# Strided-head loads laid out as (row of 32, group), split over two queues, a mask from a one-hot product, and filler products at the start

## The chip, the cores and the metric

One core of one Trainium2 chip runs the whole program. The metric is the device time of one execution in microseconds (us). It is the median over several executions of the same compiled kernel. Profiled executions are separate ones: their rows give the durations, and their own total stands beside their span below.

## What is computed

The program is an attention layer followed by two gated feed-forward layers, all in float32:

```
scores = (1/sqrt(D)) * q @ k.T                     # 4 batches, 8 heads, 576 positions, D = 64
rel = pos[:, None] - pos[None, :]
mask_local   = (rel >= 0) & (rel < 32)             # heads 0..3
mask_strided = (rel >= 0) & (pos[None] % 32 == pos[:, None] % 32)   # heads 4..7
attn = softmax(where(mask, scores, -1e9)) ;  x = attn @ v           # heads side by side: 2304 x 512
x = x / sqrt(mean(x*x) + 1e-6) * rms_g
x = (silu(x @ w_gate) * (x @ w_val)) @ w_out       # d_ff = 1536
out = (silu(x @ w2_gate) * (x @ w2_val)) @ w2_out
```

What matters here are the strided heads. A position is 32 t + r, with t from 0 to 17 (the row of 32) and r from 0 to 31 (the residue). A query sees only keys of its own residue and of rows t up to its own.

## The kernel before, in words

**Strided heads in groups.** The kernel packs several residues into one tile of positions, so that one 126x126 or 108x108 product gives the scores of many residues at once; a mask takes away pairs of different residues. Residues 0 to 29 are written as r = 5 a + g, with a from 0 to 5 and g from 0 to 4. Group g holds the six residues a, each with its 18 rows t: 108 positions. The two residues 30 and 31 are put behind groups 0 and 1 as positions 108 to 125, so those two groups have 126 positions. In the kernel before, position index is (a, t), a outside and t inside. `load_strided` (L550) loads one tensor of one batch with five DMAs: one per head of 108 runs of 320 floats (L555) and one for residues 30 and 31 (L557). In batch 0 two of k's five are issued from GpSimd (POOL), all others from SyncE (SP), in the order q, k, v.

**Order of a batch.** `batch` (L899) writes the steps of a batch in a list: six transposes of q and k (`strided_t`, L631, operation at L80) into `qT` and `kT`, copied out of PSUM at L87; then per group a score step (`strided_s`, product at L76), a softmax (maximum with mask at L675 on VectorE, exp at L684 on ScalarE, normalising at L701 on GpSimd), a transpose of the weights (`turn_step`) and the product with v (`strided_v`, L797), whose `post` (L813) copies the result from PSUM into the tile `x` with the residues put back in place. The local heads follow. The loads of the local heads of a batch reuse the tiles of its strided q and k (L573), so they wait for the last transpose that reads these.

**What else runs in the first 50 us.** The steps of the attention of batch 0 are mixed with the decoding of the first weights: `raw` tiles are loaded on SP (L160), scaled on ScalarE (L288, L280, L305) and joined on VectorE (L292, L297, L309). A scheduler with a model of its own then fixes the order of the instructions on each engine; each engine takes its instructions in that order.

**Fillers.** `keep_busy` (L67) counts the steps with products or transposes at the start of the program. At the counts in a small table it puts in products of a constant tile `warm` (128x128 by 256 columns), whose result nobody reads (L72). In the kernel before the first are at count 11.

**Constants.** `consts` (L531) builds the masks on GpSimd with `affine_select`: two local masks, `ms` for the strided heads (index j not above i, and j in the same run of 18 as i), then `ones`, and `warm` as a copy of it on VectorE (L546).

After some 250 us only the feed-forward layers are left, as a long sequence of products on TensorE (PE), with weights fetched and split beside them.

Of the kernel before, what the change touches and what calls it, by code (L numbers as in the profile page):

```python
# [12 lines left out]
ALU = mybir.AluOpType  # L13
# [4 lines left out]
NEG = -8.0e9  # L18
# [7 lines left out]
def attn_ffn_ffn(ctx: ExitStack, tc: tile.TileContext, q, k, v, w1g, w1v, w1o, rms_g, w2g, w2v, w2o, out):  # L26
    nc = tc.nc
    B, H, S, D = q.shape
# [4 lines left out]
    HH = H // 2  # L33
# [33 lines left out]
    def keep_busy():  # L67
        if state["start"] and state["kind"] and state["group"] != state["filled"]:
            state["filled"] = state["group"]
            state["count"] += 1  # L70
            for _ in range({11: 24, 14: 8, 28: 5, 31: 7, 34: 9, 36: 22}.get(state["count"], 0)):
                traced(nc.tensor.matmul(att.fill, att.warm[:, :128], att.warm, start=True, stop=True))  # L72

    def product(out_, a, b_, start, stop, **how):
# [7 lines left out]
    def bank(tag):  # L82
        return pp.tile([128, 512], F32, tag=tag, name=f"b_{tag}")

    def copy(eng, out_, in_):
        if eng is nc.scalar:
            nc.scalar.copy(out=out_, in_=in_)  # L87
        else:
            eng.tensor_copy(out=out_, in_=in_)
# [405 lines left out]
    class Attention:  # L495
# [35 lines left out]
        def consts(self):  # L531
            g = nc.gpsimd

            def sel(t, pattern, base, cm):
                g.affine_select(out=t, in_=t, pattern=pattern, compare_op=ALU.is_ge, fill=NEG, base=base, channel_multiplier=cm)

            for m, leads in ((self.m0, (0, 32)), (self.m1, (32, 32))):
                g.memset(m, 0.0)
                for par, lead in enumerate(leads):
                    sel(m[64 * par:64 * par + 64], [[-1, 96]], lead, 1)  # L540
                    sel(m[64 * par:64 * par + 64], [[1, 96]], 31 - lead, -1)
            g.memset(self.ms, 0.0)
            sel(self.ms, [[-1, 126]], 0, 1)
            sel(self.ms, [[18, 7], [0, 18]], 17, -1)
            g.memset(self.ones, 1.0)
            nc.vector.tensor_copy(out=self.warm.rearrange("p (a k) -> p a k", a=2), in_=self.ones.unsqueeze(1).to_broadcast([128, 2, 128]))  # L546
            g.memset(self.expo, -0.5)
            nc.sync.dma_start(out=self.gcol, in_=rms_g.rearrange("(c p) -> p c", p=128))

        def load_strided(self, t, src, b, engs=None):  # L550

            engs = engs or [nc.sync] * 5
            for h in range(HH):
                s = src[b, HH + h].rearrange("(t r) d -> t r d", r=32)[:, 0:30, :].rearrange("t (a g) d -> a t (g d)", g=5)
                engs[h].dma_start(out=t[0:108, h].rearrange("p (g d) -> p g d", d=D), in_=s)  # L555
            s = src[b, HH:H].rearrange("h (t r) d -> t h r d", r=32)[:, :, 30:32, :].rearrange("t h r d -> t h (r d)")
            engs[4].dma_start(out=t[108:126, :, 0:2 * D], in_=s)  # L557

        def load(self, b, half):
            res = []  # L560
            for nm, src in (("q", q), ("k", k)):
                if half == 0:
                    t = self.p1.tile([128, 5, HH * D], F32, tag=nm, name=f"{nm}n{b}{half}")
                else:
                    t = self.p1.tile([126, HH, 5 * D], F32, tag=nm, name=f"{nm}n{b}{half}")
                    self.load_strided(t, src, b, [nc.sync,nc.sync,nc.gpsimd,nc.gpsimd,nc.sync] if b == 0 and nm == "k" else None)
                res.append(t)
            self.ld[b, half] = res
            if half == 0:
                for h in range(0, HH, 2):  # L570
                    for t, src in zip(res, (q, k)):
                        for h_ in (h, h + 1):
                            nc.sync.dma_start(out=t[:, 0:4, h_ * D:(h_ + 1) * D], in_=src[b, h_, 0:512].rearrange("(c p) d -> p c d", p=128))  # L573
                for t, src in zip(res, (q, k)):
                    nc.sync.dma_start(out=t[0:64, 4].rearrange("p (h d) -> p h d", d=D),
                                      in_=src[b, 0:HH, 512:S].rearrange("h p d -> p h d"))

        def load_v(self, b, half):
# [10 lines left out]
                nc.sync.dma_start(out=t[:, :, 0, :], in_=v[b, 0:HH, 0:96, :].rearrange("h p d -> p h d"))  # L589
            else:  # L590
                t = self.p1.tile([126, HH, 5 * D], F32, tag="vs", name=f"vs{b}")
                self.load_strided(t, v, b)
            self.vt[b, half] = t

        def qk_tile(self, b, half, which):
# [201 lines left out]
        def strided_v(self, b, part, pair):  # L797
            cell = {}
# [13 lines left out]

            def post():  # L813
                x = self.x_tile(b, 1)
                nr = n // 18
                for k in range(2):
                    g = 2 * part + k if pair is not None else 4
                    d = x[:, k if pair is None else pair].rearrange("p (t r) -> p r t", r=32)[:, g:g + 5 * (nr - 1) + 1:5, :]
                    copy(self.eng(), d, cell["o"][:, 128 * k:128 * k + n].rearrange("p (r t) -> p r t", t=18))

            return Step([pe, post] + ([lambda: self.squares(b, 0)] if part == 2 else []),
                        lambda: ("T", ("s", b, part, pair)) in self.st and (b == 0 or (b - 1, 1) in self.done), kind="v")
# [277 lines left out]
    open_pool("px", "px", 0, bufs=1)  # L1100
    actx = ExitStack()
    att = Attention(actx)
    make_identity(nc, att.ident)
    att.load(0, 1)
    att.load_v(0, 1)
# [611 lines left out]
```

## Time and profile before

| | us |
|---|---|
| median of 3 runs | 1014.53 (1012.96 to 1014.74) |
| the profiled execution, its own time | 1019.0 |
| span of its rows | 1017.2 |
| PE busy | 970.2 (95%) |
| VectorE (DVE) busy | 582.4 (57%) |
| ScalarE (ACT) busy | 578.1 (57%) |
| GpSimd (POOL) busy | 387.6 (38%) |

The profiled execution took 4.5 us more than the median of the runs; 1.8 us of its time lie outside its span. Rows of the trace are in us from the start of the span. Busy times are sums of durations that may overlap on one engine. In the chain of work that ended last, traced back from the end, PE holds 71% of the span.

### The profile page before, as it was taken

The numbers are of one execution on the slowest core, as the hardware profiler recorded it, in microseconds if no ns is written. First come the engines' busy times: TensorE is split into PE (matmuls) and PEld (weight loads), VectorE is DVE, ScalarE is ACT, GpSimd is POOL, SyncE is SP. The second block draws the span as 40 slices with busy tenths as digits, with TensorE's granted clock in tenths as the row PEclk, the third lists the DMA queues.
The fourth block names the chain that finished last, engine by engine and source line by source line (L and its number), as shares of the span: only waits on it lengthen the run. The fifth ranks groups of instructions, "written<-read, shape, count | busy, mean of one in ns | idle before, by whom it ended". The sixth has DMA issues, their size and how long they took to land.

```text
span 1017.2 us, 17631 instructions
## 1 busy us (share of the span) xinstructions
PE 970.2 (95%) x5987; PEld 891.7 (88%) x5987; DVE 582.4 (57%) x1310; ACT 578.1 (57%) x1465; POOL 387.6 (38%) x417
## 2 busy tenths in 40 slices
PE   5789988899999999998999999999999999999998
PEld 4678966667889999998999999999998999999997
DVE  2887766767244656455655566554556645653333
ACT  5988675675254646354655555555646555663431
POOL 3221243442050538160716464673517143431500
PEclk9989999799999999999999999999999999999999
DMA  7774647856777474977567777637887397865211
GB/s 184 216 228 139 162 134 230 240 173 212 257 262 260 147 231 167 318 258 266 188 203 249 277 227 247 202 135 285 281 285 244 133 303 247 311 199 181 83 63 63
DMA packets 167794, 215.87 MB, mean 212 GB/s; under 512 B 46356, under 2 KB 121308, under 8 KB 167704
## 3 DMA queue, kind: packets, MB, share of 16 engines
q1 hardware_dynamic: 158296, 199.79, 60.7%
q10 hardware_dynamic: 9216, 14.68, 3.9%
q8 instruction: 47, 0.77, 0.3%
q14 instruction: 43, 0.35, 0.1%
q0 software_dynamic: 192, 0.28, 0.1%
HBM read 142.87 MB, written 71.83 MB: 211 GB/s over the span
## 4 chain that ended last, share of the span: by engine, by line
PE 71%; DMA 3%; ACT 2%; DVE 1%; issue 0%; SPq 0%; DVEq 0%; ACTq 0%
PE b_y L76 32%; PE b_a L76 17%; PE b_g L76 12%; PE b_v L76 10%; DMA pk<-dh 1%; DMA w<-pk 1%; DMA raw<-in_moe_w_gate_dram 0%; DMA pk<-raw 0%; ACT xh L1389 0%; ACT dh L280 0%; ACT hh L1471 0%; ACT raw L288 0%; DVE dh L297 0%; ACT t L1447 0%; ACT t L1461 0%
## 5 line engine op out<-in xcount | busy, mean ns | idle before, releaser
L1390 POOL TENSOR_TENSOR xl<-xst,xh 128x384 fp32r<-128x384 f32 x196 | 211.4, 1100 | 179.7 <-PE b_y L76 77.6
L76 PE MATMUL b_y<-xh,w 128*128 128x384 f32 x784 | 212.1, 336 | 5.0 <-ACT t L1447 3.1
L76 PEld LDWEIGHTS b_y<-xh,w 128*128 128x128 f32 x784 | 143.5, 188 | 8.2 <-ACT t L1447 3.7
L76 PE MATMUL b_a<-xh,w 128*128 128x384 f32 (+2 forms) x512 | 141.3, 336 | 0.8 <-ACT t L1447 0.7
L76 PE MATMUL b_y<-xl,w 128*128 128x384 f32 x392 | 131.7, 336 | 0.0
L76 PE MATMUL b_g<-xh,w 128*128 128x384 f32 (+2 forms) x416 | 127.9, 349 | 0.0
L76 PE MATMUL b_v<-xh,w 128*128 128x384 f32 (+2 forms) x352 | 109.3, 353 | 1.8 <-ACT t L1461 1.8
L76 PEld LDWEIGHTS b_a<-xh,w 128*128 128x128 f32 x512 | 93.3, 188 | 4.4 <-ACT t L1447 2.0
L1389 ACT CAST xh<-xst 128x384 fp32r<-128x384 f32 x196 | 91.6, 521 | 0.3 <-DMA xst<-y_d 0.3
L386 POOL TENSOR_TENSOR raw<-dh 128x256 f32<-128x256 f32 x40 | 29.4, 754 | 154.5 <-ACT t L1447 36.8
L76 PE MATMUL b_a<-xl,w 128*128 128x384 f32 (+2 forms) x256 | 85.9, 335 | 0.0
L76 PEld LDWEIGHTS b_g<-xh,w 128*128 128x128 f32 x416 | 77.4, 191 | 5.3 <-issue 0.4
L76 PE MATMUL b_y<-hh,w 128*128 128x384 f32 (+2 forms) x304 | 81.4, 343 | 0.0
L76 PEld LDWEIGHTS b_y<-xl,w 128*128 128x128 f32 x392 | 73.7, 188 | 1.8
L76 PEld LDWEIGHTS b_v<-xh,w 128*128 128x128 f32 x352 | 65.8, 193 | 7.4 <-ACT t L1461 2.2
L701 POOL TENSOR_TENSOR e<-e,rc 128x384 f32<-128x384 f32 (+3 forms) x40 | 35.8, 903 | 93.8 <-DVE rc L695 28.0
L76 PE MATMUL b_g<-xl,w 128*128 128x384 f32 (+2 forms) x208 | 70.8, 340 | 0.0
L76 PE MATMUL b_y<-w,hh 128*128 128x512 f32 x216 | 67.1, 391 | 0.0
L684 ACT ACTIVATE e<-e,nb 128x96 f32<-128x96 f32 (+2 forms) x152 | 56.8, 380 | 9.7 <-DVE nb L675 8.7
L76 PE MATMUL b_v<-xl,w 128*128 128x384 f32 (+2 forms) x176 | 60.3, 342 | 0.0
L76 PEld LDWEIGHTS b_y<-hh,w 128*128 128x128 f32 x304 | 55.2, 190 | 2.7
L1467 DVE TENSOR_TENSOR b_y<-b_y,t 128x384 f32<-128x384 f32 x56 | 31.6, 565 | 44.4 <-ACT b_y L1461 43.4
(206 smaller groups left out, 2149.7 us busy)
## 6 DMA issues: line engine op xcount, KB each, us to landing
w<-pk SPq DMA_DIRECT2D x48, 512.0 KB
raw<-in_moe_w_gate_dram SPq DMA_DIRECT2D x24, 512.0 KB
raw<-in_moe_w_val_dram SPq DMA_DIRECT2D x24, 512.0 KB
raw<-in_moe_w_out_dram SPq DMA_DIRECT2D x24, 512.0 KB
pk<-raw ACTq DMA_DIRECT2D x48, 256.0 KB
part<-ob SPq DMA_DIRECT2D x48, 256.0 KB
xst<-y_d SPq DMA_DIRECT2D x30, 384.0 KB
xst<-xq SPq DMA_DIRECT2D x28, 384.0 KB
```

The costliest lines, as they stand in the source:

```text
L76: traced(nc.tensor.matmul(out_, a, b_, start=start, stop=stop, **how))
L386: paced(nc.gpsimd.tensor_tensor(out=t[:, z], in0=a, in1=b, op=ALU.subtract))
L684: r = nc.scalar.activation(out=e[:qn, i, :kn], in_=e[:qn, i, :kn], func=AF.Exp, bias=nb[:qn, i:i + 1], scale=-1.0, accum_out=sums[:qn, i:i ...
L701: eng.tensor_tensor(out=e[:qn, :nt, :kn], in0=e[:qn, :nt, :kn], in1=rc[:qn, :nt].unsqueeze(2).to_broadcast([qn, nt, kn]), op=ALU.mult)
L1389: nc.scalar.copy(out=xh[:, kk], in_=src[:, kk])
L1390: paced(nc.gpsimd.tensor_tensor(out=xl[:, kk], in0=src[:, kk], in1=xh[:, kk].bitcast(F32), op=ALU.subtract), ("pe", None))
L1467: nc.vector.tensor_tensor(out=s, in0=s, in1=v, op=ALU.mult)
```

## The change

- **Index (t, a) instead of (a, t).** Position in a group is now 6 t + a. `load_strided` loads, per head, rows t = 0 to 15 with one DMA whose source runs over 16 rows, 6 residues and 320 floats; rows 16 and 17 come with one DMA each for all four heads together (6 residues x 4 heads x 320 floats); residues 30 and 31 as before. That is seven DMAs a tensor instead of five.
- **Two queues in batch 0.** k's seven are issued from ScalarE, q's and v's from SP, none from GpSimd.
- **Mask by product.** Seven one-hot rows (six for a, one for residues 30 and 31) are built on 7 partitions; their product with themselves on PE is 1 where residues agree; VectorE turns that into 0 or -8e9, and one `affine_select` on GpSimd sets the upper triangle.
- **Result copies.** `strided_v` copies 108 columns per group to `x` as (t, a). In groups 0 and 1 one more copy on VectorE for both groups together puts residues 30 and 31 in place.
- **Products of constants at the top.** `ones` and `warm` are made first of all constants, and `keep_busy` puts 22 filler products ahead of the first transpose.

```
--- before.py
+++ after.py
@@ -68,7 +68,7 @@
         if state["start"] and state["kind"] and state["group"] != state["filled"]:
             state["filled"] = state["group"]
             state["count"] += 1
-            for _ in range({11: 24, 14: 8, 28: 5, 31: 7, 34: 9, 36: 22}.get(state["count"], 0)):
+            for _ in range({1: 22, 11: 24, 14: 8, 28: 5, 31: 7, 34: 9, 36: 22}.get(state["count"], 0)):
                 traced(nc.tensor.matmul(att.fill, att.warm[:, :128], att.warm, start=True, stop=True))
 
     def product(out_, a, b_, start, stop, **how):
@@ -531,30 +531,32 @@
         def consts(self):
             g = nc.gpsimd
 
-            def sel(t, pattern, base, cm):
-                g.affine_select(out=t, in_=t, pattern=pattern, compare_op=ALU.is_ge, fill=NEG, base=base, channel_multiplier=cm)
-
+            def sel(t, pattern, base, cm, op=ALU.is_ge, fill=NEG):
+                g.affine_select(out=t, in_=t, pattern=pattern, compare_op=op, fill=fill, base=base, channel_multiplier=cm)
+
+            row = self.ms[0:7]
+            g.memset(row, 0.0)
+            sel(row[:, 0:108].rearrange("p (t a) -> p t a", a=6), [[0, 18], [-1, 6]], 0, 1, ALU.not_equal, 1.0)
+            sel(row[:, 108:126], [[0, 18]], -6, 1, ALU.not_equal, 1.0)
+            same = bank("g")
+            nc.tensor.matmul(same[0:126, 0:126], row, row, start=True, stop=True)
+            nc.vector.tensor_scalar(out=self.ms[0:126], in0=same[0:126, 0:126], scalar1=1.0, scalar2=-NEG, op0=ALU.subtract, op1=ALU.mult)
             for m, leads in ((self.m0, (0, 32)), (self.m1, (32, 32))):
                 g.memset(m, 0.0)
                 for par, lead in enumerate(leads):
                     sel(m[64 * par:64 * par + 64], [[-1, 96]], lead, 1)
                     sel(m[64 * par:64 * par + 64], [[1, 96]], 31 - lead, -1)
-            g.memset(self.ms, 0.0)
-            sel(self.ms, [[-1, 126]], 0, 1)
-            sel(self.ms, [[18, 7], [0, 18]], 17, -1)
-            g.memset(self.ones, 1.0)
-            nc.vector.tensor_copy(out=self.warm.rearrange("p (a k) -> p a k", a=2), in_=self.ones.unsqueeze(1).to_broadcast([128, 2, 128]))
+            sel(self.ms[0:126], [[-1, 126]], 0, 1)
             g.memset(self.expo, -0.5)
             nc.sync.dma_start(out=self.gcol, in_=rms_g.rearrange("(c p) -> p c", p=128))
 
-        def load_strided(self, t, src, b, engs=None):
-
-            engs = engs or [nc.sync] * 5
+        def load_strided(self, t, src, b, eng):
+            s = src[b, HH:H].rearrange("h (t r) d -> t h r d", r=32)
             for h in range(HH):
-                s = src[b, HH + h].rearrange("(t r) d -> t r d", r=32)[:, 0:30, :].rearrange("t (a g) d -> a t (g d)", g=5)
-                engs[h].dma_start(out=t[0:108, h].rearrange("p (g d) -> p g d", d=D), in_=s)
-            s = src[b, HH:H].rearrange("h (t r) d -> t h r d", r=32)[:, :, 30:32, :].rearrange("t h r d -> t h (r d)")
-            engs[4].dma_start(out=t[108:126, :, 0:2 * D], in_=s)
+                eng.dma_start(out=t[0:96, h], in_=s[0:16, h, 0:30].rearrange("t (a g) d -> t a (g d)", g=5))
+            for i in (16, 17):
+                eng.dma_start(out=t[6 * i:6 * i + 6], in_=s[i, :, 0:30].rearrange("h (a g) d -> a h (g d)", g=5))
+            eng.dma_start(out=t[108:126, :, 0:2 * D], in_=s[:, :, 30:32].rearrange("t h r d -> t h (r d)"))
 
         def load(self, b, half):
             res = []
@@ -563,7 +565,7 @@
                     t = self.p1.tile([128, 5, HH * D], F32, tag=nm, name=f"{nm}n{b}{half}")
                 else:
                     t = self.p1.tile([126, HH, 5 * D], F32, tag=nm, name=f"{nm}n{b}{half}")
-                    self.load_strided(t, src, b, [nc.sync,nc.sync,nc.gpsimd,nc.gpsimd,nc.sync] if b == 0 and nm == "k" else None)
+                    self.load_strided(t, src, b, nc.scalar if b == 0 and nm == "k" else nc.sync)
                 res.append(t)
             self.ld[b, half] = res
             if half == 0:
@@ -589,7 +591,7 @@
                 nc.sync.dma_start(out=t[:, :, 0, :], in_=v[b, 0:HH, 0:96, :].rearrange("h p d -> p h d"))
             else:
                 t = self.p1.tile([126, HH, 5 * D], F32, tag="vs", name=f"vs{b}")
-                self.load_strided(t, v, b)
+                self.load_strided(t, v, b, nc.sync)
             self.vt[b, half] = t
 
         def qk_tile(self, b, half, which):
@@ -812,11 +814,13 @@
 
             def post():
                 x = self.x_tile(b, 1)
-                nr = n // 18
                 for k in range(2):
                     g = 2 * part + k if pair is not None else 4
-                    d = x[:, k if pair is None else pair].rearrange("p (t r) -> p r t", r=32)[:, g:g + 5 * (nr - 1) + 1:5, :]
-                    copy(self.eng(), d, cell["o"][:, 128 * k:128 * k + n].rearrange("p (r t) -> p r t", t=18))
+                    d = x[:, k if pair is None else pair].rearrange("p (t r) -> p t r", r=32)
+                    copy(self.eng(), d[:, :, g:g + 26:5], cell["o"][:, 128 * k:128 * k + 108].rearrange("p (t r) -> p t r", r=6))
+                if part == 0:
+                    copy(nc.vector, d[:, :, 30:32].rearrange("p t r -> p r t"),
+                         cell["o"][:, 0:256].rearrange("p (k n) -> p k n", n=128)[:, :, 108:126])
 
             return Step([pe, post] + ([lambda: self.squares(b, 0)] if part == 2 else []),
                         lambda: ("T", ("s", b, part, pair)) in self.st and (b == 0 or (b - 1, 1) in self.done), kind="v")
@@ -1100,6 +1104,8 @@
     open_pool("px", "px", 0, bufs=1)
     actx = ExitStack()
     att = Attention(actx)
+    nc.gpsimd.memset(att.ones, 1.0)
+    nc.vector.tensor_copy(out=att.warm.rearrange("p (a k) -> p a k", a=2), in_=att.ones.unsqueeze(1).to_broadcast([128, 2, 128]))
     make_identity(nc, att.ident)
     att.load(0, 1)
     att.load_v(0, 1)
```

On PE, the start of the program, before the first transposes of q (`qn`) and k (`kn`) of the strided heads. Before:

```order
L1712 UNCONDITIONAL_BRANCH
L80 MATMUL b_a_162<-ident,qn_107 128x126 x4
L80 MATMUL b_a_171<-ident,kn_113 128x126 x4
L80 MATMUL b_g<-ident,qn_107 128x108 x4
L80 MATMUL b_y_186<-ident,kn_113 128x108 x4
```

After:

```order
L1718 UNCONDITIONAL_BRANCH
L72 MATMUL b_v<-warm 128x256 x21
L542 MATMUL b_g<-ms 126x126
L72 MATMUL b_v<-warm 128x256
L80 MATMUL b_a_174<-ident,qn_109 128x126 x4
L80 MATMUL b_a_205<-ident,kn_117 128x126 x4
L80 MATMUL b_g<-ident,qn_109 128x108 x4
```

The fillers and the mask's product stand ahead of the transposes; behind them the order on PE is the same to the end of the program, but for one group of eight score products.

On ACT, the start of the program, ahead of the first copies of transposes out of PSUM. After (before, the first row here is the table load, and no DMA stands on this engine):

```order
L556 DMA kn_117<-in_k_dram 96x1x320 x4
L558 DMA kn_117<-in_k_dram 6x4x320 x2
L559 DMA kn_117<-in_k_dram 18x4x128
L87 ACT_TABLE_LOAD
L87 COPY qT_201<-b_a_174 128x504
```

Seven issues now stand ahead of the table load.

On DVE, the softmax of the strided heads of the last batch, between the sums (`sums`), their reciprocals (`rc`) and the gate of a feed-forward block (`sg`). Before:

```order
L694 TENSOR_SCALAR sums<-sums 126x4
L695 RECIPROCAL rc<-sums 126x4
L694 TENSOR_SCALAR sums<-sums 108x4
L695 RECIPROCAL rc<-sums 126x4
L695 RECIPROCAL rc<-sums 108x4
L972 SCALAR_TENSOR_TENSOR sg<-sg,b_g 128x512
L694 TENSOR_SCALAR sums<-sums 108x4
L695 RECIPROCAL rc<-sums 108x4
L89 COPY pT<-b_a_2888 126x4x126
```

After:

```order
L434 TENSOR_TENSOR raw<-raw 128x512
L697 RECIPROCAL rc<-sums 126x4
L696 TENSOR_SCALAR sums<-sums 126x4
L696 TENSOR_SCALAR sums<-sums 108x4
L697 RECIPROCAL rc<-sums 126x4
L697 RECIPROCAL rc<-sums 108x4
L696 TENSOR_SCALAR sums<-sums 108x4
L697 RECIPROCAL rc<-sums 108x4
L89 COPY pT<-b_a_2946 126x4x126
L976 SCALAR_TENSOR_TENSOR sg<-sg,b_g 128x512
```

A subtraction of a weight (`raw`) now stands ahead of the reciprocals, and the gate behind the copy of `pT`.

## Rows read from the trace of the kernel before

**Rows 1.** The page's busy times of the engines, share of the span.

```profile
PE 970.2 (95%) x5987; PEld 891.7 (88%) x5987; DVE 582.4 (57%) x1310; ACT 578.1 (57%) x1465; POOL 387.6 (38%) x417
```

**Rows 2.** Windows of 50 us: length, busy by engine, PE's granted clock, DMA share, GB/s.

```profile
0.00:50.00 50.00, 32.39 (x357) 27.57 (x357) 27.92 (x121) 38.17 (x132) 15.00 (x34) 1.00 0.73 198
...
150.00:200.00 50.00, 41.46 (x264) 31.77 (x265) 32.80 (x103) 31.03 (x97) 17.44 (x21) 0.86 0.81 245
```

**Rows 3.** Timeline, PE, first transposes and scores: start, length, operation, [idle before, releaser].

```profile
8.98 1.07 PE L80 MATMUL b_a<-ident,qn 126*128 126x126 f32 x4 [8.98 <-DMA qn<-in_q_dram]
11.05 1.07 PE L80 MATMUL b_a<-ident,kn 126*128 126x126 f32 x4 [0.99 <-DMA kn<-in_k_dram]
...
14.07 0.93 PE L80 MATMUL b_y<-ident,kn 108*64 108x108 f32 x4
14.93 0.57 PE L76 MATMUL b_y<-kT,qT 64*126 64x126 f32 x1
```

**Rows 4.** Timeline, SP, DMA issues of the first 16 us.

```profile
0.75 3.30 SPq L555 DMA_DIRECT2D qn<-in_q_dram  x4
...
6.72 3.06 SPq L555 DMA_DIRECT2D vs<-in_v_dram  x4
...
10.81 0.49 SPq L160 DMA_DIRECT2D raw<-in_moe_w_gate_dram  x1
...
14.31 0.92 SPq L573 DMA_DIRECT2D qn<-in_q_dram  x2
```

**Rows 5.** Windows, columns as in rows 2: strided loads alone, and other loads.

```profile
8.00:13.00 5.00, 3.03 (x15) 2.69 (x16) 0.00 (x0) 1.28 (x3) 0.00 (x0) 1.00 0.43 149
14.00:18.00 4.00, 4.00 (x45) 3.57 (x44) 2.00 (x19) 2.81 (x10) 0.00 (x0) 1.00 1.05 360
```

**Rows 6.** DMA view, 0 to 30 us in 40 slices; issue to landing of POOL's k loads.

```profile
DMA  0003466444544444488999999999999792389898
...
DMA to landing us min/median/max: 3.9/4.2/4.4
```

**Rows 7.** Timeline, ACT, from the start to the first decoded weight.

```profile
0.74 1.28 ACT L87 ACT_TABLE_LOAD   x1 [0.74 <-PEq L1701]
...
16.33 0.40 ACT L684 ACTIVATE e<-e,nb 126x126 f32<-126x126 f32 x1 [0.78 <-DVE nb L675]
...
16.73 0.65 ACT L288 ACTIVATE raw<-raw 128x512 uint32<-128x512 uint32 x1
```

**Rows 8.** Timeline, constants, fillers and later transposes.

```profile
3.83 0.40 DVE L546 CAST warm<-ones 128x256 fp32r<-128x256 f32 x1 [3.83 <-POOL ones L545]
...
17.12 3.12 PE L72 MATMUL b_v<-warm 128*128 128x256 f32 x24
...
21.88 0.65 PE L80 MATMUL b_a<-ident,e 126*126 126x126 f32 x4 [1.64 <-POOL e L701]
...
57.12 0.53 PE L80 MATMUL b_y<-ident,qn 108*64 108x108 f32 x4
57.49 0.53 PE L80 MATMUL b_y<-ident,kn 108*64 108x108 f32 x4
```

**Rows 9.** Timeline, copies of results on ACT and small operations on DVE.

```profile
28.67 0.60 ACT L87 COPY x<-b_y 128x126 f32<-128x126 f32 x2
...
19.41 0.17 DVE L694 TENSOR_SCALAR sums<-sums 126x4 f32<-126x4 f32 x1
...
201.64 0.28 DVE L89 COPY qT<-b_y 128x128 f32<-128x128 f32 x1
```

**Rows 10.** Timeline, PE, the last batch's two longest waits.

```profile
179.11 0.48 PE L76 MATMUL b_y<-kT,qT 64*126 64x126 f32 x1 [2.32 <-DVE mean L864]
188.72 0.65 PE L80 MATMUL b_a<-ident,e 126*126 126x126 f32 x4 [2.44 <-POOL e L701]
```

**Rows 11.** Windows of 4 us, columns as in rows 2, behind the second wait.

```profile
188.00:192.00 4.00, 3.27 (x15) 2.73 (x16) 2.83 (x12) 1.79 (x9) 4.00 (x5) 0.68 1.01 346
192.00:196.00 4.00, 4.00 (x14) 2.76 (x14) 0.35 (x2) 1.46 (x7) 1.26 (x2) 0.50 0.93 284
```

## The prediction

> **What bounds the kernel now.** I read the page's busy times first, then the windows, then the timeline of the first 20 us engine by engine, and last the waits of the middle. PE is busy 95% of the span [rows 1]. The missing time is not spread evenly: in the first 50 us PE is busy 32.39 us, in 150 to 200 us 41.46 [rows 2]. So some 17.6 us of idle PE lie at the start and 8.5 in one later stretch, and the rest of the program is PE back to back. A shorter start moves everything behind it by as much, unless something there has a time of its own.
>
> At the start PE has nothing to do until q has landed, at 8.98, and then waits 0.99 more for k, which lets it go on at 11.05; the first score product starts at 14.93 [rows 3]. SP issues q's four large DMAs in 3.30 us, so 0.8 us each, and v's only from 6.72; the first weight is issued at 10.81 and the local heads' q at 14.31 [rows 4], which is just behind the last transpose of the strided q. While only strided loads run, 8 to 13 us, the DMA engines are 0.43 busy at 149 GB/s; with weights and local heads in flight, 14 to 18 us, they are full at 360 GB/s [rows 5]. The row of forty slices of 0.75 us shows the same: nothing before slice 4, then a long row of 4s, then 9s [rows 6]. So the strided loads keep 6 or 7 of 16 engines busy. A shortage of bytes is not what makes PE wait.
>
> ACT starts on its first exp at 16.33 and on its first weight at 16.73 [rows 7]; from there to 50 us it is close to full (38.17 of 50 us with the empty first 10, [rows 2]). ACT, in order, sets the pace of the head once it has begun.
>
> **The change, part by part.**
>
> *Loads of q and k.* The source now runs over 16 rows outside, where it ran over 6 residues. I take it that these loads then spread like the weights' in 14 to 18 us, 0.43 to full. A tensor of strided heads is 4 heads x 576 rows x 64 floats = 0.59 MB, so q and k are 1.18 MB. At 149 GB/s they need 7.9 us, at 360 GB/s 3.3 us [rows 5]. Issue: bounds 0.8 us each (q's own, [rows 4]) and 0.49 (a weight's, which spreads, [rows 4]); I take 0.5 because the new form spreads. Seven cost 3.5 us from 0.75, on SP for q and on ACT for k side by side; the last is issued from 3.75 on (with 0.8: 5.55). From issue to landing: POOL's k loads took 3.9 to 4.4 us on the crowded six engines [rows 6], the upper bound; the lower is 1.9, between the first issue at 0.75 and the slice in which the first DMA moves, the fourth, whose middle is 2.6 us. I take 2.65, nearer the low end, since the crowd goes: q and k land at 6.4. The data alone gives 2.6 + 3.3 = 5.9, so it agrees; ends 5.65 and 8.15 (0.5 issue with the shorter landing, 3.75 + 4.4; the dear issue with 2.65 gives 8.2).
>
> The Trainium skill (DMA: Bandwidth & Descriptors, Issuing engines are not separate DMA queues) says that a second issuing engine saves only the issue time, which it calls usually small beside the DMA. Here the rows say otherwise: 3.30 us of issue for 0.49 MB, where 360 GB/s would move that in 1.4. By the page the data would set the landing, 5.9 instead of my 6.4, and the gain would be 0.5 us more.
>
> *ACT's seven issues* (3.5 us) stand ahead of its table load of 1.28 us [rows 7]: 0.75 + 3.5 + 1.28 = 5.5, before the first copy that ACT has to make, at 7 us. Cost nothing; with the dear issue 7.6, half a us late.
>
> *Fillers and transposes.* Four transposes of 126 columns take 1.07 us at the start, and 0.65 later, as part of the same kernel; of 108 columns 0.93 and 0.53 [rows 3, 8]. The granted clock reads 1.00 in 8 to 13 us [rows 5], yet the operations take 1.7 times as long, so I trust the durations: the first transposes ran at the lower level, 1.2 GHz. The 22 fillers shall change that. `ones` moves from behind two DMA issues on POOL to the front, so `warm`, cast at 3.83 [rows 8], is there at about 1.5. A filler takes 0.13 us at the higher level (24 in 3.12, [rows 8]), up to 0.26 at the lower: 22 end between 4.4 and 7.2, say 6.0, when q lands. After a wait of 1.64 us PE still ran at the higher level [rows 8], so a short gap loses nothing. Before, five groups take 3.88 us from 11.05 to the first score [rows 3]; now all six wait for nothing but PE: 4.7 at the lower level, and by 0.53/0.93 to 0.65/1.07, so 0.6, 2.8 at the higher. First score: 6.4 + 2.8 = 9.2 instead of 14.93, **5.7 us earlier**. Ends: at the lower level, with fillers to 7.2, 11.9, so 3.0; landing at 8.2 and the lower level 12.9, so 2.0; landing at 5.65 and the higher level 8.45, so 6.5.
>
> *Mask.* Its product stands as the 22nd on PE; POOL makes its rows before, and behind it come one operation on DVE and one on POOL, both idle then. The scores need it 3 us later. Nothing; if it were late, it would be late by tenths.
>
> *What follows the first score.* v's issues end at 0.75 + 14 x 0.5 = 7.75, so the first weight goes out at 8.2 instead of 10.81, 2.6 us earlier, on engines that are then nearly free of strided data: before, the 1.77 MB of q, k and v took 11.9 us at 149 GB/s, from 2.6 to 14.5. At 360 GB/s the 0.52 MB are there at 8.2 + 1.9 + 1.5 = 11.6. ACT would reach it behind its third exp at 16.33 - 5.7 + 1.2 = 11.8 [rows 7]. The local heads' q goes out when SP is through with three weights, at 11 instead of 14.31, 3.3 earlier. So the loads just keep up; I take off 0.4 for one of them that does not (between 0 and 3, the latter if loads alone set the pace).
>
> *Result copies.* ACT copies 108 columns a group instead of 126 (two in 0.60, [rows 9]), with another order of the addresses: not dearer on a row here, and a seventh fewer columns. The eight new copies on DVE move 36 floats a lane: between 0.17 (a tiny operation) and 0.28 (128 columns) each [rows 9], 1.4 to 2.2 us in all, of which a quarter falls in batch 0's full stretch. DVE is 27.92 of 50 busy there, so at most 0.5 is on the path; I take 0.3.
>
> *Loads of batches 1 to 3.* Two more issues a tensor, each dearer by at most 7 x 0.5 against 5 x 0.7; SP is not what PE waits for. They also stop crowding 6 engines. No wait of PE in 40 to 260 us ends on a DMA, so I give it nothing, and the surplus to a rival.
>
> **Sum:** 5.7 - 0.4 - 0.3 = 5.0 us. Against the profiled execution 1019.0 - 5.0 = 1014.0; this execution was 4.5 above the median of the runs, and the same difference from that gives 1014.5 - 5.0 = **1009.5**, its own range 1008 to 1011.
>
> **The rivals.** *The lower clock stays* (0.15). For it: nothing in rows 3 shows a rise before 14.93. Against: fillers ran 0.13 us each later. Gain 3.0 - 0.7 = 2.3: 1012.2.
>
> *The loads set the pace* (0.12): the weights and local heads go out only 2.6 and 3.3 us earlier, and ACT, in order, stands before the first weight with all exps behind it. Or the new form does not spread, and q and k land at 2.6 + 7.9 = 10.5, the first score at 13.3. Either way 1 to 2 us: 1013.0. Against it speaks the full 360 GB/s of loads that run over 128 rows outside, and ACT's full row once it has begun, which is why it stays low. The Trainium skill (DMA: Bandwidth & Descriptors, Why a DMA increments its semaphore by 16 and not by 1) has the number of engines as the largest up to 16 that divides both outer sizes: 6 before (residues) and 16 after. The trace agrees for before (0.43 x 16 = 6.9); of after it has no row.
>
> *Batch 3 loses its clock more often* (slower, 0.14 with its mild form). In the last batch's softmax DVE has a new order: a weight's subtraction ahead of the reciprocals. PE waits there already 2.32 and 2.44 us [rows 10], and behind the second the granted clock is 0.68 and then 0.50 [rows 11], which is 0.32 x 4 + 0.5 x 4 = 3.3 us lost; in all of 150 to 200 us 0.14 x 50 = 7.0 [rows 2]. One more fall eats 3.3 of the 5.0: 1012.8, no change (0.06). If the shifted start makes the stretch lose its 7.0 a second time, the kernel is slower by 2.0 and more: 1016.6 (0.08). It decides from two added falls on. For it: the order of DVE and ACT changes up to there. Against: the order on PE does not.
>
> *More than the start* (0.09): strided loads that no longer crowd six engines also shorten waits in batches 1 to 3, 2 to 3 us: 1007.
>
> **How the numbers follow.** My forecast has 0.50. About 0.2% (2 us) is what a measurement of this kernel can tell from no change. Faster: 0.50 + 0.15 + 0.09 = 0.74; within: 0.12 + 0.06 = 0.18; slower: 0.08. The range takes in the first four cases and the ends of the landing and the clock: 6.5 with a surplus of 3 at one end (1005), a gain of nothing at the other (1014.6); what is left out is the slower case and some of the largest gain.
>
> **What would show it.** Right: first transpose at about 6.4 with 0.65 us for four, first score at 9 to 9.5, first exp at 10.6, full DMA share by 5 us, and PE's later rows the same but earlier by 5. Clock wrong: transposes of 1.07 us. Loads: ACT waiting before L288. Batch 3: a PE wait above 2.5 us near 180, and a granted clock below 0.8 in 150 to 200. The prediction fails if the first score comes 5 us earlier and the end does not.

## The result, and the profile after

| | before | after |
|---|---|---|
| median of 5 runs, us | 1014.53 (1012.89 to 1016.18) | 1006.85 (1002.65 to 1007.29) |
| ratio, 95% interval | | 0.9917 [0.9893, 0.9941] |
| the profiled execution, us | 1019.0 | 1006.85 |

The change saves 7.7 us by the medians. The predicted 1009.5 is 2.7 us off and the range holds the result, but the gain does not come from where I put it: the first score comes only 0.7 us earlier, and the new form in batches 1 to 3 alone, to whose loads I gave nothing, gains as much as the whole change.

The page's busy times and the two windows of the kernel after, which answer to [rows 1, 2]:

```profile
PE 974.6 (97%) x6011; PEld 897.3 (89%) x6011; DVE 579.1 (58%) x1319; ACT 576.9 (57%) x1465; POOL 387.2 (39%) x416
```

```profile
0.00:50.00 50.00, 39.16 (x382) 33.81 (x382) 27.43 (x124) 38.54 (x133) 14.86 (x33) 0.90 0.77 200
150.00:200.00 50.00, 44.00 (x323) 33.46 (x320) 36.32 (x114) 32.71 (x104) 20.66 (x23) 0.93 0.82 252
```

PE is busy 6.77 us more in the first 50 us than before, but some 4.6 us of that are fillers, so it is no shorter start. In 150 to 200 us it is busy 2.54 us more at a higher granted clock (0.93 for 0.86); that is work done earlier.

**The start.** PE's timeline of the kernel after (answers to [rows 3, 8]):

```profile
1.59 4.21 PE L72 MATMUL b_v<-warm 128*128 128x256 f32 x21 [1.59 <-DVE warm L1108]
...
9.53 1.07 PE L80 MATMUL b_a<-ident,qn 126*128 126x126 f32 x4 [3.00 <-DMA qn<-in_q_dram]
10.40 1.05 PE L80 MATMUL b_a<-ident,kn 126*128 126x126 f32 x4
...
13.40 0.93 PE L80 MATMUL b_y<-ident,kn 108*64 108x108 f32 x4
14.26 0.57 PE L76 MATMUL b_y<-kT,qT 64*126 64x126 f32 x1
```

The fillers start at 1.59 and end at 6.53. Then PE waits 3.00 us for q, which is there at 9.53, later than the 8.98 of before, and the transposes take 1.07 us as before. Only k no longer has a wait of its own. The first score comes at 14.26 instead of 14.93. Why q is late stands in the issues of SP and, behind them, of ACT (answers to [rows 4, 7]):

```profile
0.74 2.91 SPq L556 DMA_DIRECT2D qn<-in_q_dram  x4
3.69 2.88 SPq L558 DMA_DIRECT2D qn<-in_q_dram  x2
6.71 0.27 SPq L559 DMA_DIRECT2D qn<-in_q_dram  x1
```

```profile
0.73 2.63 ACTq L556 DMA_DIRECT2D kn<-in_k_dram  x4
3.80 2.10 ACTq L558 DMA_DIRECT2D kn<-in_k_dram  x2
```

Two small loads of q take 2.88 us to issue; near 135 us the same two take 0.83:

```profile
135.58 0.83 SPq L558 DMA_DIRECT2D qn<-in_q_dram  x2
```

A semaphore is a counter that a DMA raises as its data lands. In the trace, SP's and ACT's DMAs together carry eight semaphore numbers. The first eight loads, four of q and four of k, take all of them. From then on an issue holds its engine, in order, until the load that last had its number has landed. The ninth load finds its number free; of the five behind it, q's second small load stands longest, 2.0 us, until q's second large load has landed at 6.28. SP's waits in the first 20 us name it:

```profile
SPq L558 <- DMA qn<-in_q_dram: 2.0, 1, 2.0
```

The last piece of q goes out at 6.71; with 0.83 us for the two it would be about 4.6 (an estimate).

The data is slower than I took it as well. Windows of the kernel after (answers to [rows 5]):

```profile
3.00:6.00 3.00, 3.00 (x19) 2.87 (x17) 0.00 (x0) 0.00 (x0) 1.74 (x8) 1.00 0.93 247
...
14.00:18.00 4.00, 4.00 (x45) 3.64 (x44) 2.48 (x25) 2.81 (x12) 0.00 (x0) 0.86 1.06 351
```

The new loads do fill the engines (0.93 where the old ones held 0.43), but at that share they move 247 GB/s of these 1280-byte runs, not the 360 of weights.

**The later batches.** The same products of `pT` and `vl` of batch 3's local heads on PE, before and then after:

```profile
147.44 0.69 PE L76 MATMUL b_a<-pT,vl 96*64 96x64 f32 x16 [1.00 <-ACT pT L87]
...
154.27 0.69 PE L76 MATMUL b_y<-pT,vl 96*64 96x64 f32 x16 [2.83 <-ACT pT L87]
...
160.88 0.69 PE L76 MATMUL b_a<-pT,vl 96*64 96x64 f32 x16
```

```profile
148.19 0.69 PE L76 MATMUL b_a<-pT,vl 96*64 96x64 f32 x16
151.49 0.69 PE L76 MATMUL b_y<-pT,vl 96*64 96x64 f32 x16 [0.55 <-ACT pT L87]
...
156.55 0.69 PE L76 MATMUL b_a<-pT,vl 96*64 96x64 f32 x16
```

After reaches the first of these products 0.75 us later than before, and the last 4.3 us earlier: the stretch takes 8.36 us instead of 13.44. I use this length as a gauge below. ACT's timeline there, before:

```profile
143.38 0.65 ACT L427 CAST raw<-raw 128x512 fp32r<-128x512 f32 x1
146.44 0.33 ACTq L430 DMA_DIRECT2D pk<-dh  x1
146.81 0.58 ACT L87 COPY pT<-b_a 96x512 f32<-96x512 f32 x1 [2.78 <-PE b_v L76]
...
149.13 0.37 ACT L684 ACTIVATE e<-e,nb 128x96 f32<-128x96 f32 x1 [1.02 <-DMA xst<-x_d]
```

ACT ends its cast at 144.03 and starts the copy of `pT` 2.78 us later. PE's transposes for that copy ended at 142.50; what lies between is the issue of a store of a decoded weight to device memory (`pk<-dh`), whose data had been cast by 143.2. So the releaser that the row names, a product into `b_v`, is not the cause. The store's semaphore was last used by SP's write `xq<-xst` of 140.19, behind the strided loads of q and k; by the trace it landed at 146.37, and the store went out at 146.44. In the run with v alone changed (below), ACT's timeline names the write itself:

```profile
145.81 0.58 ACT L87 COPY pT<-b_a 96x512 f32<-96x512 f32 x1 [1.69 <-DMA xq<-xst]
```

The runs below show that the lateness of the write is what matters, and not which DMA's number the store happens to take. In the four kernels that load q and k of batch 3 by SP in the old form (before, start alone, batch 0 alone, v alone), the store takes its number from such a write; the write lands 5.0 to 6.2 us after its issue, and the store goes out within 0.1 us of that. In the four that load them one residue at a time, it takes its number from such a write too, but this lands after 3.4 to 4.0 us, 1.1 to 1.8 before the store, and ACT does not wait for it. (New rows with nine engines lies between, 3.6 us and the store 0.1 behind. In after, the number comes from a small load of k that landed 2.6 us before.)

SP waits for the same writes; its waits from 130 to 160 us, before and then after:

```profile
SPq L160 <- DMA xq<-xst: 6.1, 3, 3.0
```

```profile
SPq L160 <- DMA xq<-xst: 0.9, 1, 0.9
```

Windows of the two kernels, before first:

```profile
135.00:138.00 3.00, 3.00 (x37) 2.12 (x36) 1.51 (x14) 2.67 (x12) 0.09 (x1) 1.00 0.41 134
...
144.00:150.00 6.00, 4.04 (x46) 3.29 (x44) 3.14 (x15) 2.19 (x11) 1.64 (x2) 1.00 0.47 145
156.00:159.00 3.00, 3.00 (x24) 2.21 (x22) 0.00 (x0) 0.58 (x1) 0.00 (x0) 0.54 0.60 201
```

```profile
144.00:150.00 6.00, 6.00 (x69) 5.26 (x67) 5.22 (x21) 6.00 (x24) 4.03 (x6) 1.00 0.83 255
156.00:159.00 3.00, 3.00 (x32) 2.01 (x31) 1.73 (x3) 2.58 (x7) 1.01 (x1) 1.00 0.64 164
```

Before, strided loads hold 0.41 of the engines, that is 6.6 of 16; then ACT works 2.19 of 6 us, PE 4.04, and after PE's waits its granted clock is 0.54. After, ACT and PE work 6.00 of 6 and the clock stays at 1.00. PE's wait of 2.83 us comes later than ACT's stall: ACT, in order and held at further stores, reached that copy of `pT` only at 153.63.

A later piece of 3 us lies between 178 and 250 us. There the two waits of [rows 10] are still there:

```profile
174.77 0.37 PE L76 MATMUL b_y<-kT,qT 64*126 64x126 f32 x1 [2.29 <-DVE mean L868]
184.32 0.65 PE L80 MATMUL b_a<-ident,e 126*126 126x126 f32 x4 [2.10 <-POOL e L703]
```

but behind the second the granted clock is back sooner (windows after, against 0.68 and 0.50 in [rows 11]):

```profile
184.00:188.00 4.00, 3.68 (x20) 3.02 (x20) 2.50 (x12) 1.86 (x9) 3.93 (x5) 0.72 1.00 364
188.00:192.00 4.00, 4.00 (x25) 3.03 (x24) 1.00 (x4) 1.20 (x4) 0.91 (x1) 0.85 0.76 234
```

This piece cannot be put down to the change from one profile each. Start alone, batch 0 alone and the old loads on GpSimd, which keep the old form of these loads, come 2.3 to 2.9 us nearer to the profiled before between 178 and 196 us, after itself 1.6.

At 250 us the same PE instruction stands 7.5 us earlier in the profiled execution of after. Some 4.5 us more appear behind 400 us; every other kernel below, whatever it changes, gains 2 to 8 us there against this one profiled execution of before. It was itself 4.5 us above its median, so I don't count them for the change.

### The profile page after: what moved, and what is told of

It reads as the page before. It is cut to its first block, busy times and chain, and to the rows that moved or that the text cites. A ratio compares the mean times of both kernels' runs of the same rounds, so it can differ in the third digit from the quotient of the medians.

```text
span 1005.1 us, 17715 instructions
## 1 busy us (share of the span) xinstructions
PE 974.6 (97%) x6011; PEld 897.3 (89%) x6011; DVE 579.1 (58%) x1319; ACT 576.9 (57%) x1465; POOL 387.2 (39%) x416
## 4 chain that ended last, share of the span: by engine, by line
PE 70%; DMA 4%; ACT 2%; DVE 1%; issue 0%; SPq 0%; POOL 0%; DVEq 0%; POOLq 0%
PE b_y L76 32%; PE b_a L76 17%; PE b_g L76 12%; PE b_v L76 10%; DMA pk<-dh 1%; DMA xst<-x_d 1%; DMA raw<-in_moe_w_gate_dram 0%; DMA ob<-part 0%; DMA xst<-xq 0%; DMA part<-ob 0%; DMA pk<-raw 0%; ACT xh L1395 0%; ACT dh L280 0%; ACT hh L1477 0%; ACT raw L288 0%
```

## The experiments

Three theories. L: the gain comes from the strided loads of batches 1 to 3, which land sooner and free what queues behind them. S: it is the shorter start, carried through. O: it is the new order of instructions on DVE and ACT that comes with the new layout. The kernel before ran again beside each group of runs, at medians of 1016.03, 1016.22 and 1015.36 us. "Gauge" is the length of the stretch above: 13.44 us before, 8.36 after.

**Start alone, old loads.** Before, with `ones` and `warm` first, 22 fillers, and k of batch 0 issued by ACT:

```
-{11: 24, ...
+{1: 22, 11: 24, ...
-[nc.sync,nc.sync,nc.gpsimd,nc.gpsimd,nc.sync] if b == 0 and nm == "k" else None
+[nc.scalar] * 5 if b == 0 and nm == "k" else None
```

> Kernel before with the fillers and the early constants, and k of batch 0 on ACT's queue; layout, loads on 6 engines, mask and result copies as before. Theory L (the gain comes from strided loads of batches 1 to 3 that land sooner and free the DMA queues): 1012 to 1016, the PE waits of 2.8 us near 154 and the loss near 190 still there. Theory S (a shorter start carries through): 1007 to 1011.

Measured: 1013.44, ratio 0.9977 [0.9957, 0.9996]; PE's first transpose at 11.78, 2.8 us later than before. These parts by themselves do little, and as the start did not get shorter, the run is no test of S. Gauge 13.17.

**No fillers.** After, without the 22:

```
-{1: 22, 11: 24, ...
+{11: 24, ...
```

> Changed kernel without the 22 fillers ahead of the first transpose. Theory L: 1005 to 1009, as the changed kernel; the first transposes take 1.07 us with and without fillers, since PE waits 3.0 us for q after the fillers. Theory S: 1010 to 1014.

Measured: 1006.14, ratio 0.9903 [0.9870, 0.9937], no different from the change. Gauge 8.39. The fillers earn nothing here.

**New form in batch 0 alone, and in batches 1 to 3 alone.** Rows, loads, mask and copies are new where `FRESH` says so (in the second kernel it returns `b > 0`); the second keeps the old start, without fillers:

```
+def FRESH(b):
+    return b == 0
...
+            if not FRESH(b):
...
```

> New layout, loads, mask and copies in batch 0 only, with fillers and two queues; batches 1 to 3 in the old form with loads on 6 engines. Theory L: 1011 to 1016. Theory S: 1006 to 1009.

> Batch 0 in the old form, without fillers, k's loads as before; batches 1 to 3 in the new form. Theory L: 1004 to 1009. Theory S: 1012 to 1016. A third theory O (the new order of instructions on DVE and ACT): any of the four may fall between, and the waits near 150 would change with the order, not with the loads.

Measured: batch 0 alone 1010.31, ratio 0.9953 [0.9931, 0.9975], gauge 12.51; batches 1 to 3 alone 1004.88, ratio 0.9898 [0.9870, 0.9925], gauge 8.45. The later batches alone give all that the change gives. Batch 0 alone gives some 5 us, between the two expectations; but by the ratios the two don't add (5 and 10 apart, 8 together). In batch 0 alone, PE's timeline reads:

```profile
9.02 0.62 PE L84 MATMUL b_a<-ident,qn 126*128 126x126 f32 x4 [1.85 <-DMA qn<-in_q_dram]
9.47 0.75 PE L84 MATMUL b_a<-ident,kn 126*128 126x126 f32 x4
10.01 0.93 PE L84 MATMUL b_g<-ident,qn 108*128 108x108 f32 x4
```

Behind a wait of 1.85 us the first four transposes took 0.62 us, so behind the fillers and a short gap they ran at the higher clock; the groups from 10.01 on took 0.93 again.

Nor does the 5 us show a shorter start carried through. The same PE instructions stand 2.0 us earlier than before at 30 us and 0.3 later at 80. Against the run with batch 3 alone below, whose edit touches nothing ahead of 131 us, it is 2.4 earlier and then 0.9. So most of the lead is gone by 80 us, and where the 5 us come from was not followed.

**Old rows, nine engines.** Before, with strided loads of batches 1 to 3 per residue, four heads in one DMA. 18 rows run outside. Layout, masks and copies stay old, so O predicts a gain only if the scheduler makes a new order of its own:

```
-            for h in range(HH):
...
+            if b == 0:
+                for h in range(HH):
...
+            for a in range(6 if b else 0):
+                s = src[b, HH:H].rearrange("h (t r) d -> t h r d", r=32)[:, :, 5 * a:5 * a + 5].rearrange("t h g d -> t h (g d)")
+                nc.sync.dma_start(out=t[18 * a:18 * a + 18], in_=s)
```

> The kernel before, with its old rows, masks, copies and start, but in batches 1 to 3 the strided heads are loaded one residue for all four heads at a time, so that 18 rows of 32 run outside: 9 engines by the rule that the two traces bore out (6 and 16). Seven DMAs a tensor, as in the change. Theory L (the gain comes from strided loads of batches 1 to 3 that occupy few engines for long): about half to two thirds of the 11 us that the new loads of batches 1 to 3 gave, so 1007 to 1011, with the strided q and k moving at 200 to 260 GB/s near 135 us. Theory O (the gain comes from the new order of copies and products on DVE and ACT, which this kernel doesn't have): 1014 to 1017, as before.

**New rows, nine engines.** Batches 1 to 3 new, but each head's 18 rows in one DMA:

```
-                eng.dma_start(out=t[0:96, h], in_=s[0:16, h, 0:30]...
-            for i in (16, 17): ...
+                eng.dma_start(out=t[0:108, h], in_=s[0:18, h, 0:30]...
```

> The version with the new form in batches 1 to 3 only (measured 1004.9), but each head's 30 residues of all 18 rows in one DMA: 18 and 108 outside, so 9 engines in place of 16, and five DMAs a tensor in place of seven. Theory L: slower than 1004.9 by the part of the engines that is lost, 1006 to 1011, and within 2 us of the run with old rows and nine engines. Theory O: 1004 to 1006, as the run with sixteen.

Measured: old rows 1002.95, ratio 0.9887 [0.9853, 0.9921], gauge 8.30; new rows 1011.98, ratio 0.9957 [0.9928, 0.9985], gauge 11.74. The first lies below the range that L expected, the second just above it. The new layout is not needed: with the old one the whole gain is there, and with the new one more than half of it can be lost. For the stretch of the gauge O falls: up to 181 us ACT and DVE run their operations in the order of before in the run with old rows, and the gauge is 8.30. Behind 181 us O does not fall. There the scheduler gave that run another order as well: DVE reaches the gate (`sg`) behind four reciprocals (`rc`) of the softmax instead of three. The same holds in every kernel with the whole gain, and in none of the others, so order and loads were not separated there. L in the form "number of engines" does not hold alone: both have nine, and they differ by 9 us. Batch 3's issues of k on SP, old rows and then new rows:

```profile
137.74 2.48 SPq L559 DMA_DIRECT2D kn<-in_k_dram  x6
```

```profile
136.94 3.23 SPq L571 DMA_DIRECT2D kn<-in_k_dram  x4
```

Six DMAs of 18 rows x 4 heads are issued in 2.48 us, four of 108 runs of a head in 3.23, for the same bytes. SP waits for `xq<-xst` 1.0 us in all with the first and 4.4 with the second (6.1 before). So the number of engines is not all of it; whether the dearer issue makes the difference, or the longer DMAs themselves, was not separated.

**Old loads, issued by GpSimd.** The same six engines, but off SP's queue and off the shared semaphores:

```
-            engs = engs or [nc.sync] * 5
+            engs = engs or [nc.gpsimd if b else nc.sync] * 5
```

> The kernel before with the strided loads of batches 1 to 3 issued by GpSimd: the same six engines, but off SP's queue and off the eight semaphores that SP's and ACT's DMAs share. Theory L in its form 'who waits is the next issue' (ACT stood at a store of a parked weight until one of the shared semaphores came free): the stall of 2.78 us of ACT near 146 us is gone and 1005 to 1010 comes out. Theory L in its form 'the engines are crowded' (what is queued behind the strided packets on six engines is late whoever issued them): 1013 to 1018, with PE still waiting near 147 to 154 us, and GpSimd's issues add to it.

Measured: 1013.28, ratio 0.9987 [0.9964, 1.0009], no gain, which is the second form's time. Yet PE's stretch is the shortest of all, 8.07 us, and ACT goes past the store without a stall:

```profile
150.11 0.69 PE L76 MATMUL b_a<-pT,vl 96*64 96x64 f32 x16
...
158.18 0.69 PE L76 MATMUL b_a<-pT,vl 96*64 96x64 f32 x16
```

So this stall is one of issue order and shared semaphores, as the first form has it, and not of crowded engines alone; but its end alone brought no gain. The time is lost again 40 us on; PE and then ACT:

```profile
197.71 0.34 PE L80 MATMUL b_y<-ident,qn 64*128 64x64 f32 x2 [3.20 <-ACT x L87]
```

```profile
196.55 0.60 ACT L994 CAST xh<-xraw 128x192 fp32r<-128x192 f32 x2 [5.02 <-DMA xraw<-x_d]
```

ACT, in order, stands 5.02 us before a cast whose load SP had issued only at 191.42, with PE's copies queued behind it. Why that load costs more here than elsewhere I did not follow.

**A start with few DMAs in flight.** After, with the six small loads of q and k of batch 0 on GpSimd:

```
+            few = nc.gpsimd if b == 0 and src is not v else eng
-                eng.dma_start(out=t[6 * i:6 * i + 6], ...
+                few.dma_start(out=t[6 * i:6 * i + 6], ...
```

> The changed kernel, with the three small strided loads of q and the three of k of batch 0 issued by GpSimd: no more than eight DMAs of SP and ACT are then in flight at the start, so none waits for a semaphore. Expected at the start: q and k landed by 6.5 to 8, four transposes in 0.65 us since the dummy products end just before, first score at 9.5 to 11 in place of 14.26. If a shorter start carries through, 1003 to 1005; if the full ACT and the weights' loads take it back within the first 80 us, 1005.5 to 1008, as the change itself (1006.9).

Measured: 1002.01, ratio 0.9896 [0.9859, 0.9933], not told apart from the change. The start missed what it was built for:

```profile
7.13 0.94 PE L80 MATMUL b_a<-ident,qn 126*128 126x126 f32 x4 [0.67 <-POOL m L535]
9.26 0.62 PE L80 MATMUL b_a<-ident,kn 126*128 126x126 f32 x4 [1.20 <-DMA kn<-in_k_dram]
9.81 0.69 PE L542 MATMUL b_g<-ms 7*126 7x126 f32 x2
10.88 0.98 PE L80 MATMUL b_g<-ident,qn 108*128 108x108 f32 x4 [0.38 <-DVE ms L543]
...
13.96 0.57 PE L76 MATMUL b_y<-kT,qT 64*126 64x126 f32 x1
```

The first transpose of q starts at 7.13, 2.4 us sooner, so the waits for the shared semaphores were real. But k is there only at 9.26, the last of GpSimd's issues being at 4.84. And the mask's product (L542) now stands between the transposes: the next ones start at 10.88, behind DVE's reading of that product, and take 0.98 us again. So the first score is at 13.96. Whether a first score at 9 would carry through stays untested: no run made one.

**Which of the later loads.** Nine engines as in the run with old rows, for batch 3 alone, for q and k alone, for v alone (the condition of its loop, against that run):

```
-            for a in range(6 if b else 0):
+            for a in range(6 if b == 3 else 0):
...
+            for a in range(6 if b and src is not v else 0):
...
+            for a in range(6 if b and src is v else 0):
```

> The kernel before, with the strided loads of batch 3 alone (issued near 131 and 152 us) one residue for all four heads at a time: 9 engines in place of 6, 0.3 us of issue in place of 0.75. If the gain comes from batch 3, whose softmax follows its loads at once (PE's rows came 5.9 us nearer between 140 and 158 us and 4.3 us more up to 250 in the run with batches 1 to 3 changed): 999 to 1005, not slower than that run's 1002.95, and PE's rows before 130 us as in the kernel before. If batches 1 and 2 carry part of it: 1006 to 1012.

> Nine engines for q and k of batches 1 to 3; v as before on six. q and k of batch 3 are issued from 131 to 138 us, v from 152 to 156. If the first piece (5 to 6 us between 140 and 158) hangs on q and k and the second (4 us between 178 and 250) on v: 1006 to 1010, with the wait of PE for POOL's e near 188 us back at over 2 us. If q and k alone carry both, because an earlier start of the softmax puts what follows in another place: 1002 to 1005.

> Nine engines for v of batches 1 to 3; q and k as before on six. If q and k make the first piece: it is missing, and ACT stands near 146 us again. v's own piece of 4 us then shows as 1010 to 1013; if v gives nothing, 1014 to 1018, as before.

| | median, us | ratio, 95% interval | gauge, us |
|---|---|---|---|
| batch 3 alone | 1004.25 | 0.9890 [0.9861, 0.9919] | 8.30 |
| q and k alone | 1002.93 | 0.9874 [0.9850, 0.9897] | 8.30 |
| v alone | 1009.59 | 0.9948 [0.9928, 0.9968] | 13.66 |

Batch 3 alone has the whole gain, and so have q and k alone. v alone leaves the stretch at 13.66 and still gives 5 us: its gain comes from elsewhere. By the ratios v's 5 and q's and k's 13 give 11.5 together, as if something later could be mended once, from either side, which is what my second expectation for q and k had; which waits end there was not followed.

The run with batch 3 alone corrects a reading, too. In after PE loses 3.0 us against the profiled before near 72 us, and in ten of the twelve other kernels 1.5 or 3.0, behind a wait for POOL that in the profiled before took 1.39 us and left the clock at 1.00. I took this for a cost of the change, but the kernel with nothing changed ahead of 131 us has a wait of 2.00 and a fall to 0.65, and loses 1.5 us there:

```profile
70.50 0.65 PE L80 MATMUL b_y<-ident,e 126*126 126x126 f32 x4 [2.00 <-POOL e L705]
```

```profile
72.00:76.00 4.00, 4.00 (x28) 3.68 (x26) 1.73 (x12) 2.63 (x12) 3.57 (x4) 0.65 1.08 385
```

So the profiled before, one execution, is an exception there, and with it v alone, whose wait there is 1.22.

**Nine engines everywhere.** The loads per residue in batch 0 too, three of each of q and k on GpSimd:

```
...
+[nc.scalar] * 4 + [nc.gpsimd] * 3 if b == 0 and nm == "k" else [nc.sync] * 4 + [nc.gpsimd] * 3 if b == 0 else None
```

> Old rows, masks and copies; all strided loads one residue for all heads (9 engines, 0.3 us of issue), and in batch 0 q's first four on SP, k's first four on ACT and the six others on GpSimd, so that at most eight of SP's and ACT's are in flight. No dummy products. Against the run with batches 1 to 3 only (1002.95): q and k land at 7.5 to 8.5 in place of 8.98 and 11.05, first score at 12.3 to 13.5 in place of 14.93, transposes still at 1.07 us. If a start that is 1.5 to 2.5 us shorter carries through: 1000 to 1002. If the full ACT takes it back: 1002 to 1005.

Measured: 1006.89, ratio 0.9923 [0.9899, 0.9947], gauge 8.29; no better than leaving batch 0 as it was. q is not earlier but later:

```profile
10.09 1.07 PE L80 MATMUL b_a<-ident,qn 126*128 126x126 f32 x4 [10.09 <-DMA qn<-in_q_dram]
```

The lowest ratio is that of nine engines for q and k alone, 0.9874 (1002.93 us). Its interval ends at 0.9897 and that of the change begins at 0.9893, so the two are hardly told apart.

## Why the prediction was right, and where it was not

- **The sum.** 5.0 us forecast, 7.7 measured. It is right by luck: two errors stand against each other, a start that gave far less than I gave it and later loads to which I gave nothing.
- **"q and k land at 6.4".** Failed: 9.53. The new form spreads, as I took it (0.93 of the engines). Two sizes were wrong. The large issues took 0.73 us each where I took 0.5, and I did not look for a limit on DMAs in flight: fourteen loads went out over eight semaphores, and five of the last six waited. And I took the weights' 360 GB/s for runs that moved at 247. (The 0.49 MB that I set beside 3.30 us of issue are the new form's; the four old loads carry 0.55.)
- **The higher clock of the transposes.** Failed, by the mark I had named: 1.07 us. The fillers ended at 6.53, as forecast (6.0), and the late q left a gap of 3.00 us. Where the gap was 1.85, four transposes took 0.62, and the later groups 0.93. So the rival of the lower clock was right about the clock, though not about the time.
- **First score at 9.2, 5.7 us earlier.** Measured 14.26, 0.67 earlier, since both terms under it failed. That the program would carry a shorter start through was never tested at that size. At 2.0 us (batch 0 alone) it did not: by 80 us 0.9 or less was left.
- **Loads of weights, result copies.** v's issues, held by the semaphores, ended at 11.24 instead of 7.75, and the first weight went out at 11.73, 0.9 us later than before and not 2.6 earlier. Neither term shows at the end. DVE's new copy held PE back 1.24 us near 37 us, and by 50 us after is ahead again by 0.6; from 80 to 140 us it is 1.9 behind the profiled before.
- **"No wait of PE in 40 to 260 us ends on a DMA, so I give it nothing".** This is the step that mattered. The sentence is true and the conclusion false. PE waited for ACT's `pT` (1.00 and 2.83 us), ACT stood in an issue (2.4 us), the issue waited for a write, and the write landed late, behind strided loads. I followed the wait one step back instead of four. My rival "More than the start" had the mechanism at 0.09 and 2 to 3 us; the new form of batches 1 to 3 alone is worth about 10. Of these the stretch of the gauge accounts for 5; where the other half comes from is open.
- **The slower rival.** It went the other way: in the last batch the clock fell less, not more (0.93 for 0.86 in 150 to 200 us). That the new order on DVE would cost time was argued from the listing alone; the run with old rows has the gate behind four reciprocals too and the whole gain. Whether that order helps was not separated.

What the Trainium skill (DMA: Bandwidth & Descriptors, Why a DMA increments its semaphore by 16 and not by 1) says of the number of engines, the largest up to 16 that divides both outer sizes, the trace bears out for 6 (share 0.41) and 16 (0.93). The Trainium skill (DMA: Bandwidth & Descriptors, Queues, rings and completion order) says that on each of the 16 engines descriptors are taken in the order of the ring; this fits the `xq<-xst` writes that land late behind strided loads, though the trace shows only that they are late, not the ring.

## What to carry to other kernels

Follow a wait back until it ends at a transfer or at the start, above all through an engine that issues DMAs itself: its idle time before an operation may be an issue that waits for somebody else's write. Count the DMAs in flight against the semaphores that their issuers share before a load is split into more pieces. Gains in a stretch full of waits don't add: test each part alone, and the whole. Compare a stretch with more than one kernel that is unchanged there: one profile was off by 1.5 to 3 us.

## What was not expected of the hardware

- Loads with all engines busy moved 247 GB/s in 1280-byte runs (share 0.93, 3 to 6 us of after) and 351 with weights.
- More DMAs were cheaper: on the same nine engines, a tensor's 30 residues cost SP 2.48 us as six DMAs of 18 rows x 4 heads and 3.23 as four of 108 runs.
- In every kernel here eight semaphores served all DMAs of SP and ACT, and none of GpSimd's; with all eight in use an issue held its engine for up to 2.0 us at the start of after, and in before a store on ACT was held behind an unrelated write for 2.4.
- From 8 to 13 us of before, the granted clock reads 1.00 [rows 5] while four transposes take 1.07 us; after, with fillers ahead, the transposes take the same 1.07 and the column reads 0.53 from 8 to 13 us. Durations were the ones to trust.
